# The planner of an attention and max-out FFN kernel gets other step durations, paces and margins

## The chip, the cores and the metric

The kernel runs on one core of one Trainium2 chip. The metric is the device time of one launch in microseconds (us). The median of the runs is given, beside one profiled execution whose trace is read here.

## What is computed

Windowed attention for 8 batches of 8 heads (576 positions, head size 64), followed by an FFN with the maximum of three up projections:

```python
scores = scale * np.matmul(q, k.transpose(0, 1, 3, 2))
rel = pos[:, None] - pos[None, :]
mask_plain = (rel >= 0) & (rel < 32)                       # heads 0 to 3
mask_dil = (rel >= 0) & (rel < 32 * 4) & (rel % 4 == 0)    # heads 4 to 7
scores = np.where(masks[None], scores, -1e9)
attn = np.exp(scores - np.max(scores, axis=-1, keepdims=True))
attn = attn / (np.sum(attn, axis=-1, keepdims=True) + 1e-09)
x = np.matmul(attn, v)                 # to (8 * 576 tokens, 512)
h = np.maximum(np.maximum(x @ w1, x @ w2), x @ w3)   # 512 to 768
out = h @ w_out                                       # 768 to 512
```

All is float32. The kernel keeps that accuracy by splitting each operand of the large products into a high part and a low part (`fp32r`) and adding three products: high by high, high by low, low by high.

## The kernel before

**Attention units.** The 4608 tokens are cut into 16 halves of 288 tokens. A half has four units (`attention(u, wait)`, 64 in all), each a pair of heads: two units with the plain window, two with the dilated one. A unit loads `raw` (its queries and keys) and `v`; casts `raw` to `F` and subtracts for the low parts (`qlow`, `klow`); multiplies (`scores`, tile `s`); adds the mask (`masked`) and reduces (`summed`); takes exponentials with their sums (`expo`, L578); adds 1e-9 and inverts (`eps`, `recip`); normalises (`norm`); transposes on VectorE into `PT` (`turn`, L684); multiplies by `v` (`values`, tile `pv`); and writes the high part `xH` and the low part `xL` of the result. The first 12 units are "lean": they multiply plain float32 on TensorE, with queries laid out in padded tiles `q`, and need no cast. The first eight transpose on TensorE (tile `pt`).

`xH` and `xL` are rings of four halves, so a half can be written only when the up matmuls of the tile that read the half four places earlier are done.

**Weights.** There are 24 up weights (`j` from 0 to 23, four for each of six groups `f` of 128 hidden columns) and 12 down weights. Each arrives as 64-bit words into a staging tile `st` and is put together by a chain: a load on SP; `rebias` (ACT, or DVE) into the PSUM bank `c`; `low3` (POOL, or DVE); `joined` and `sign` on DVE into a tile `c` of the tag `tmp`; `split` into the high part (`wupH` or `wdn`; ACT, DVE or POOL); a subtraction into the low part (`wupL` or `wdn`; POOL, or DVE). Each `rebias` and `low3` follows the `rebias` of the weight before, and the bank `c` has one buffer.

**FFN.** There are 12 tiles of 384 tokens. A tile has 54 up steps of four matmuls (six groups `f`, three projections, three products; tile `u`) and 18 down steps of three matmuls (tile `d`). Between them DVE takes maxima in `tmp`, and ACT and POOL split the result into `h`. Tile 0 needs units 0 to 7 and all weights; tile 1 needs units 8 to 11 too, tile 2 units 12 to 15. Three tiles use up four halves.

**The order.** Every piece of work is a `Step` with a table of engines that may run it and an assumed duration on each; the first is its usual engine. `Plan.deadlines` gives each step a due time: FFN steps on TensorE follow each other at their assumed durations times `FFN_PACE`; the steps before them are dated back along the dependencies, each by its duration times `UNIT_PACE` or `WEIGHT_PACE`, with a margin (`UNIT_SLACK`, `WEIGHT_SLACK`) and a lead per unit or weight ahead of the FFN. FFN steps on TensorE have the due time 1e6 (they fill in behind all attention), FFN steps on other engines -1e3 (they go first). `Plan.order` then simulates the engines with the assumed durations: it always takes the step that can start earliest, and among those the one due first. An engine other than the usual one takes a step only if the usual one would end it more than `SPILL` later. A result is assumed to be ready `AFTER` its engine's duration, and `TO_PE` later for TensorE. A TensorE step after a 3.4 us interval with little work is assumed to take twice as long. The instructions are issued in the order that comes out; on the chip, each engine then runs its own in that order and waits where an input isn't ready.

Of the kernel before, what the change touches and what calls it, by code (L numbers as in the profile page):

```python
# [38 lines left out]

STAGE_F, STAGE_H = 13, 3  # L40

SPILL = 2
TO_PE = 0.26
FFN_PACE = 1.267
UNIT_PACE, UNIT_SLACK, UNIT_LEAD = 1.146, 3.85, 3.484
WEIGHT_PACE, WEIGHT_SLACK, WEIGHT_LEAD = 0.89, 0, 0.8


def blocks_of(hf, dil):
# [54 lines left out]
class Plan:  # L104
# [1 line left out]

    AFTER = {"pe": 0.3, "act": 0.2, "dve": 0.2, "pool": 0.2, "sp": 0.0}

    def __init__(self):
        self.steps = []
# [35 lines left out]
    def order(self):  # L148
        self.deadlines()
        free = {"pe": 0.6, "act": 4.0, "dve": 4.3, "pool": 3.6, "sp": 0.6}  # L150
        wire = 0.0
        busy = {}
        slots = {b.tag: [(0.0, i) for i in range(b.limit)] for st in self.steps for b in st.bufs}
        waiting = {e: [] for e in free}
        for st in self.steps:
            if not st.left:
                for e in st.costs:
                    waiting[e].append(st)
        order = []
        while len(order) < len(self.steps):  # L160
            best = None
            for e, cands in waiting.items():
                now = free[e]
                for st in cands:
                    at = max(now, st.ready[e])
                    if best is not None and at > best[0]:
                        continue
                    for b in st.bufs:
                        if b.slot is None:
                            at = max(at, min(slots[b.tag], default=(1e9,))[0])  # L170
                    if best is not None and (at, st.due) >= best[:2]:
                        continue
                    if e != st.usual:
                        u = st.usual
                        queue = sum(
                            o.costs[u]
                            for o in waiting[u]
                            if o.due < st.due and o.usual == u and o.ready[u] <= at
                        )
                        if max(free[u], st.ready[u]) + queue + st.costs[u] < at + st.costs[e] + SPILL:  # L180
                            continue
                    best = (at, st.due, e, st)
            at, _, e, st = best
            assert at < 1e9, "the steps wait for each other's buffers"
            for b in st.bufs:
                if b.slot is None:
                    free_slot = min(slots[b.tag])
                    b.slot = free_slot[1]
                    slots[b.tag].remove(free_slot)
            if e == "sp":  # L190
                free[e] = at + 0.48
                wire = max(wire, at + 1.1) + st.nbytes / 360e3
                end = wire + 1.0
            else:
                cost = st.costs[e]
                if e == "pe":

                    tick = int(at / TICK)
                    if busy.get(tick - 1, 0) < 3060:
                        cost *= 2  # L200
                    end, cols = at + cost, st.costs[e] * 2400 * st.rows / 128
                    while tick * TICK < end:
                        part = min(end, (tick + 1) * TICK) - max(at, tick * TICK)
                        busy[tick] = busy.get(tick, 0) + cols * part / cost
                        tick += 1
                end = free[e] = at + cost
            st.eng = e
            order.append(st)
            for o in st.costs:
                waiting[o].remove(st)  # L210
            for b in st.bufs:
                b.users -= 1
                b.end = max(b.end, end)
                if not b.users:
                    slots[b.tag].append((b.end + 0.2, b.slot))
            for n in st.next:
                n.left -= 1
                for o in n.costs:
                    if e == o:
                        lat = 0.0 if e == "pe" else 0.13  # L220
                    else:
                        lat = self.AFTER[e] + (TO_PE if o == "pe" else 0.0)
                    n.ready[o] = max(n.ready[o], end + lat)
                if not n.left:
                    for o in n.costs:
                        waiting[o].append(n)
        return order
# [9 lines left out]
def tile_dilated_window_attention__then__maxout_ffn(  # L237
# [49 lines left out]
    plan = Plan()  # L287
# [44 lines left out]
    def tt(eng, dst, a, b, op):  # L332
        (nc.vector if eng == "dve" else nc.gpsimd).tensor_tensor(dst, a, b, op=op)  # L333

    def act(n):
        return 0.15 + 0.00071 * n

    def dve(n):
        return 0.065 + n / 960

    def dve2(n):
        return 0.07 + n / 1920

    def pool1(n):
        return 0.165 + n / 1200

    def pool(n):
        return 0.06 + 0.00235 * n


    NWU = 4 * NF
# [4 lines left out]
    def weight(j, before):  # L356
# [70 lines left out]
            bufs=[st],  # L427
            nbytes=NCH * n,
        )
        first = plan.add({"act": act(n), "dve": dve(n)}, rebias, [s, before], [st, cp])  # L430
        s = plan.add({"pool": pool1(n), "dve": dve(n)}, low3, [s, before], [st])
        s = plan.add({"dve": dve(n)}, joined, [s, first], [st, cp])
        s = plan.add({"dve": dve(n)}, sign, [s], [st, cp, cb])
        s = plan.add({"act": act(n), "dve": dve2(n), "pool": pool1(n)}, split, [s], [cb, *res])
        l = plan.add(
            {"pool": pool(n), "dve": dve(n)},
            lambda e: tt(e, part(1), like(cf()), part(0).bitcast(F32), ALU.subtract),
# [6 lines left out]
    def attention(u, wait):  # L444
# [32 lines left out]
        for j in range(0 if lean else 2):  # L477
            raw, F = buf("raw", f"raw{u}_{j}"), buf("F", f"F{u}_{j}")
            Fs.append(F)

            def load(_, raw=raw, j=j):
                nc.sync.dma_start(out=raw.t[:, :w], in_=qk_src[hf, dil][b, 2 * (p % 2) + j])

            def qlow(e, raw=raw, F=F):
                tt(e, F.t[64:, :HALF], raw.t[64:, :HALF], F.t[64:, :HALF].bitcast(F32), ALU.subtract)

            def klow(e, raw=raw, F=F):
                tt(e, F.t[:, w : w + ksz], raw.t[:, HALF:w], F.t[:, HALF:w].bitcast(F32), ALU.subtract)

            s = plan.add({"sp": 0.5}, load, bufs=[raw], nbytes=512 * w)  # L490
            s = plan.add(
                {"act": act(w), "dve": dve2(w), "pool": pool1(w)},
                lambda e, raw=raw, F=F: copy(e, F.t[:, :w], raw.t[:, :w]),
                [s],
                [raw, F],
            )
            parts.append(
                [
                    plan.add({"pool": pool(HALF), "dve": dve(HALF)}, qlow, [s], [raw, F]),
                    plan.add({"pool": pool(ksz), "dve": dve(ksz)}, klow, [s], [raw, F]),  # L500
                ]
            )
# [22 lines left out]
        for g, grp in enumerate(groups):  # L525
# [50 lines left out]
            def expo(_, n, nk, mo):  # L576
# [3 lines left out]
                )  # L580

            s = plan.add(
                {"pe": sum((4 if lean else 2) * x[3] / 2400 + 0.004 for x in info)},
                scores,
                [x for j in heads for x in parts[j]],
                [bank, *dict.fromkeys(Fs[j] for j in heads), *([qb] if lean else [])],
# [3 lines left out]
            if not lean:  # L590
                nn = sum(x[3] for x in info)
                s = plan.add(
                    {"dve": dve(nn) if info[0][3:] == info[1][3:] else dve(nn) + 0.065},
                    masked,
                    [s],
                    [bank, W],
# [1 line left out]
            for z, (_, i) in enumerate(grp):  # L598
                n, (nk, mo) = n0 + z, blocks[i][3:]
                t = plan.add(  # L600
                    {"dve": dve(nk) + 0.01},
                    lambda _, n=n, z=z, nk=nk, mo=mo, f=summed: f(_, n, z, nk, mo),
                    [s],
                    [bank, W, mx],
                )
                expd.append(
                    plan.add(
                        {"act": act(nk) + 0.15},
                        lambda _, n=n, nk=nk, mo=mo, f=expo: f(_, n, nk, mo),
                        [t],  # L610
                        [W, mx, sm],
# [5 lines left out]
        if not hf:  # L617
# [2 lines left out]
                a = W3() if dil else W.t[:, :768].rearrange("p (j c) -> p j c", j=2)  # L620
                nc.gpsimd.memset(a[:, :, :WIN], 0.0)

            cleared = plan.add({"pool": 0.06 + 0.00088 * (256 if dil else 64)}, clear, [expd[0]], [W])

        PT = buf("PT", f"PT{u}")
        copied, normed = [], []
# [2 lines left out]
        def inverse(n0, n1):  # L629
# [7 lines left out]
            def recip(_):  # L637
                nc.vector.reciprocal(sm.t[:nq, n0:n1], sm.t[:nq, n0:n1])  # L638

            r = plan.add({"pool": 0.075}, eps, expd[n0:n1], [sm])  # L640
            return plan.add({"dve": 0.106}, recip, [r], [sm])

        apart = half < APART
        both = None if apart else inverse(0, 2 * nb)
        for j in range(2):
# [7 lines left out]

            r = inverse(n0, n1) if apart else both
            n = nb * (wk - k0)
            done = plan.add({"pool": 0.06 + 0.00195 * n, "dve": dve(n)}, norm, [r, cleared], [W, sm])
            normed.append(done)
            if not turned:
                bank = buf("pt", f"pt{u}_{j}")
# [4 lines left out]
                            bank.t[:wk, nq * i : nq * i + nq], W3()[:nq, n0 + i], ident[:nq, :nq]  # L664
                        )

                s = plan.add({"pe": nb * (nq / 1200 + 0.003)}, transposes, [done], [W, bank], rows=nq)
                copied.append(
                    plan.add(
                        {"act": act(HALF), "dve": dve(HALF)},  # L670
# [30 lines left out]
                        stop=True,  # L701
                    )

        s = plan.add({"pe": 2 * nb * (nq / 1000 + 0.01)}, values, [vload, *copied], [v, PT, pv], rows=0.8 * wk)
        r0 = (half * HALF) % RING

        def view(ap):
# [19 lines left out]
    def ffn(t0, n, x_of, w_of, prev):  # L727
# [4 lines left out]
        for f in range(NF):  # L732
            tmp, hb = buf("tmp", f"tmp{t0}_{f}"), buf("h", f"h{t0}_{f}")
            for g in range(3):
                bank = buf("ffn", f"u{t0}_{f}_{g}")
                terms = ((wupH, 0, 0), (wupH, 0, 1), (wupL, 1, 0))
                for m, (wt, wz, xz) in enumerate(terms):

                    def up(_, m=m, wt=wt, xz=xz, f=f, g=g, bank=bank):
# [7 lines left out]
                            )  # L747

                    prev = plan.add(
                        {"pe": 4 * n / 2400 + 0.011},  # L750
                        up,
                        [
                            prev,
# [17 lines left out]
                        [bank, tmp],  # L771
                    )
            a = plan.add(
                {"act": act(n), "dve": dve2(n), "pool": pool1(n)},
                lambda e, tmp=tmp, hb=hb: copy(e, hb.t[:, 0, :n], tmp.t[:, :n]),
                [s],
                [tmp, hb],
# [12 lines left out]
        for s0 in range(0, n, 128):  # L790
            bank, o = buf("ffn", f"d{t0}_{s0}"), buf("o", f"o{t0}_{s0}")
            for f in range(NF):

                def down(_, f=f, s0=s0, bank=bank):
# [8 lines left out]

                cols = range(NWU + 2 * f, NWU + 2 * f + 2)
                prev = plan.add(
                    {"pe": 0.649},
                    down,
                    [prev, *hsteps[f], *(x for j in cols for x in w_of[j][:2])],
                    [bank, hs[f], wdn[f]],
# [97 lines left out]
```

## Time and profile before

| | |
|---|---|
| median of 3 runs | 789.0 us (787.82 to 789.14) |
| the profiled execution | 788.89 us, span from first to last instruction 787.1 us |
| TensorE (PE) busy | 737.6 us, 94% of the span |
| VectorE (DVE) busy | 455.6 us, 58% |
| ScalarE (ACT) busy | 383.7 us, 49% |
| GpSimd (POOL) busy | 408.9 us, 52% |
| mean granted TensorE clock | 0.970 of full speed |
| HBM read and written | 62.36 MB and 9.44 MB |

In the trace, a record is one instruction with its start and length; PEld is the loading of weights into TensorE. Names such as `tmp<-u` say what is written from what, with buffer numbers left out. L333, L326 and L328 are the lines of helpers, so subtractions and copies are told apart by their tiles.

### The profile page before, as it was taken

The page shows a single profiled execution, that of the slowest core. Times are in us where ns is not written, and L with a number is a line of the kernel's source. Part 1 is how long each engine was busy: PE and PEld are TensorE (multiplying, and loading weights), DVE is VectorE, ACT ScalarE, POOL GpSimd, SP SyncE. Part 2 cuts the span into 40 slices and gives each one's busy share as a digit, 9 for nine tenths or more (in the row PEclk, how much of TensorE's full clock was granted, in tenths as well). Part 3 has the DMA queues.
Part 4 walks back from the last instruction along what each step waited for, and adds up shares of the span by engine and source line. Part 5 has one row for each costly group of instructions (what it writes and reads, how often), then busy time and mean ns, then how long its engine had stood idle before and what let it go on. Part 6 is the DMA issues. An engine that isn't in the chain of part 4 may idle for free.

```text
span 787.1 us, 14709 instructions
## 1 busy us (share of the span) xinstructions
PE 737.6 (94%) x4724; PEld 673.0 (86%) x4724; DVE 455.6 (58%) x1840; ACT 383.7 (49%) x1323; POOL 408.9 (52%) x586
## 2 busy tenths in 40 slices
PE   6679776999999989999999999999999999999998
PEld 5578764898799789899799798899799899899996
DVE  6779998854886896212886887311887721011110
ACT  7776775772667656311467666511377421111111
POOL 5788998892489567411289576711088411011010
PEclk9969975999999999999999999999999999999999
DMA  6985443432433532300432542300243200100001
GB/s 196 271 255 155 131 144 122 146 95 65 129 95 98 169 101 83 101 1 3 128 106 92 157 127 67 104 28 1 81 123 106 67 29 0 41 1 14 28 1 40
DMA packets 41516, 72.75 MB, mean 92 GB/s; under 512 B 4320, under 2 KB 15584, under 8 KB 41440
## 3 DMA queue, kind: packets, MB, share of 16 engines
q1 hardware_dynamic: 41440, 71.81, 29.9%
q8 instruction: 38, 0.62, 0.3%
q14 instruction: 38, 0.31, 0.1%
HBM read 62.36 MB, written 9.44 MB: 91 GB/s over the span
## 4 chain that ended last, share of the span: by engine, by line
PE 61%; DVE 14%; ACT 4%; POOL 3%; issue 2%; DMA 1%; ACTq 0%; POOLq 0%; DVEq 0%
PE u L741 45%; PE d L796 11%; DVE PT L684 9%; PE s L545 3%; POOL F L333 2%; ACT W L578 2%; PE pv L696 2%; DVE xL L333 1%; ACT F L326 1%; DVE W L572 1%; DVE W L558 1%; POOL W L333 1%; DVE F L333 1%; DMA raw<-in_qk_p_dram 1%; DVE tmp L333 0%
## 5 line engine op out<-in xcount | busy, mean ns | idle before, releaser
L333 DVE TENSOR_TENSOR tmp<-u,tmp 128x384 f32<-128x384 f32 x144 | 80.0, 555 | 235.0 <-PE u L741 231.5
L333 POOL TENSOR_TENSOR F<-raw,F 64x288 fp32r<-64x288 f32 (+2 forms) x193 | 165.5, 858 | 71.0 <-issue 39.2
L578 ACT ACTIVATE W<-W,mx 96x128 f32<-96x128 f32 (+2 forms) x448 | 167.3, 375 | 71.9 <-DVE mx L572 71.2
L333 POOL TENSOR_TENSOR h<-tmp,h 128x384 fp32r<-128x384 f32 x72 | 73.6, 1022 | 225.7 <-ACT h L326 225.0
L741 PE MATMUL u<-xH,wupH 128*128 128x384 f32 x864 | 188.0, 339 | 0.0
L741 PE MATMUL u<-xH,wupL 128*128 128x384 f32 x864 | 187.9, 338 | 0.0
L741 PE MATMUL u<-xL,wupH 128*128 128x384 f32 x864 | 187.8, 338 | 0.0
L796 PE MATMUL d<-wdn,h 128*128 128x512 f32 x648 | 167.1, 404 | 1.3 <-DVE cp L412 0.7
L741 PEld LDWEIGHTS u<-xH,wupH 128*128 128x128 f32 x864 | 152.8, 190 | 1.5 <-issue 0.2
L741 PEld LDWEIGHTS u<-xH,wupL 128*128 128x128 f32 x864 | 152.7, 190 | 0.6 <-POOL wupL L333 0.3
L741 PEld LDWEIGHTS u<-xL,wupH 128*128 128x128 f32 x864 | 152.7, 190 | 0.2
L796 PEld LDWEIGHTS d<-wdn,h 128*128 128x128 f32 x648 | 119.6, 191 | 27.9 <-POOL wdn L333 2.5
L684 DVE STREAM_TRANSPOSE PT<-W 32x192 f32<-32x192 f32 (+1 forms) x336 | 134.7, 401 | 13.8 <-PE pv L696 7.0
L333 POOL TENSOR_TENSOR W<-W,sm 96x384 f32<-96x384 f32 (+2 forms) x121 | 96.7, 811 | 19.9 <-DVE sm L638 13.3
L326 ACT CAST h<-tmp 128x384 fp32r<-128x384 f32 x72 | 36.9, 513 | 143.9 <-DVE tmp L333 143.3
L578 ACT ACTIVATION_READ_ACCUMULATOR W<-W,mx 72x1 f32 (+1 forms) x448 | 85.0, 190 | 0.0
L326 ACT CAST F<-raw 128x576 fp32r<-128x576 f32 (+2 forms) x102 | 72.0, 706 | 9.5 <-DMA raw<-in_qk_p_dram 4.6
L572 DVE CUSTOM_DVE_ANT_0 W<-W,s 96x128 f32<-96x128 f32 (+3 forms) x364 | 75.8, 251 | 1.4
L545 PE MATMUL s<-F 128*96 128x256 f32 (+3 forms) x364 | 60.2, 271 | 16.7 <-DVE mx L572 9.2
L545 PEld LDWEIGHTS s<-F 128*72 128x72 f32 (+1 forms) x364 | 47.0, 154 | 29.6 <-issue 10.9
L558 DVE TENSOR_TENSOR W<-s,mask 72x208 f32<-72x208 f32 (+2 forms) x158 | 53.9, 360 | 25.1 <-PE s L545 23.4
L696 PEld LDWEIGHTS pv<-PT,v 104*64 104x64 f32 (+1 forms) x896 | 38.2, 145 | 32.7 <-issue 13.9
(47 smaller groups left out, 479.6 us busy)
## 6 DMA issues: line engine op xcount, KB each, us to landing
raw<-in_qk_d_dram SPq DMA_DIRECT2D x28, 352.0 KB
st<-in_w_up_dram SPq DMA_DIRECT2D x24, 384.0 KB
out_dram<-o SPq DMA_DIRECT2D x36, 256.0 KB
raw<-in_qk_p_dram SPq DMA_DIRECT2D x28, 304.0 KB
raw<-in_qk_p_dram SPq DMA_DIRECT2D x24, 288.0 KB
raw<-in_qk_d_dram SPq DMA_DIRECT2D x24, 288.0 KB
v<-in_v_d_dram SPq DMA_DIRECT2D x32, 208.0 KB
v<-in_v_p_dram SPq DMA_DIRECT2D x32, 192.0 KB
```

Source lines behind the costliest of these rows:

```text
L326: nc.scalar.copy(dst, src)
L333: (nc.vector if eng == "dve" else nc.gpsimd).tensor_tensor(dst, a, b, op=op)
L545: nc.tensor.matmul(bank.t[:nq, 256 * z : 256 * z + 2 * nk], f[:, q0 : q0 + nq], kv[:, :, k0 : k0 + nk], start=True, stop=True,)
L558: nc.vector.tensor_tensor(W3()[:nq, n0 : n0 + 2, mo : mo + nk], s3[:, :, :nk], m, op=ALU.add)
L572: nc.vector.tensor_tensor_reduce(a, x, y, -0.125, 3e38, ALU.add, ALU.min, mx.t[:nq, n : n + 1])
L578: nc.scalar.activation(a, a, AF.Exp, bias=mx.t[:nq, n : n + 1], scale=-1.0, accum_out=sm.t[:nq, n : n + 1])
L684: nc.vector.transpose(PT.t[c : c + 32, : 2 * nb, 32 * i : 32 * i + 32], W3(e)[32 * i : 32 * i + 32, :, c - e : c - e + 32],)
L696: nc.tensor.matmul(pv.t[64 * j : 64 * j + 64, q0 : q0 + nq], v.t[:wk, j, i, :], PT.t[:wk, nb * j + i, :nq], start=True, stop=True,)
L741: nc.tensor.matmul(bank.t[:, :n], wt[:, 3 * f + g, c, :], (xL if xz else xH)[:, c, r0 : r0 + n], start=(m == 0 and c == 0), stop=(m == 2 a ...
L796: nc.tensor.matmul(bank.t, hs[f].t[:, hz, s0 : s0 + 128], wdn[f].t[:, wz], start=(f == 0 and m == 0), stop=(f == NF - 1 and m == 2),)
```

## The change

The assumed durations, the margin per result (`AFTER`), the assumed DMA rate and the constants of the due times get other numbers. Nothing else of the code differs: the steps, their dependencies, buffers and instructions are the same. The plan made from them can differ in the order of the steps and in the engine of a step that may run on several.

```diff
-SPILL = 2
+SPILL = 2.0
-FFN_PACE = 1.267
-UNIT_PACE, UNIT_SLACK, UNIT_LEAD = 1.146, 3.85, 3.484
-WEIGHT_PACE, WEIGHT_SLACK, WEIGHT_LEAD = 0.89, 0, 0.8
+FFN_PACE = 0.982
+UNIT_PACE, UNIT_SLACK, UNIT_LEAD = 1.754, 6.852, 3.484
+WEIGHT_PACE, WEIGHT_SLACK, WEIGHT_LEAD = 0.535, 26.965, 0.8
...
-    AFTER = {"pe": 0.3, "act": 0.2, "dve": 0.2, "pool": 0.2, "sp": 0.0}
+    AFTER = {"pe": 0.27, "act": 0.12, "dve": 0.06, "pool": 0.12, "sp": 0.0}
...
-                wire = max(wire, at + 1.1) + st.nbytes / 360e3
+                wire = max(wire, at + 1.1) + st.nbytes / 275e3
...
-                        lat = 0.0 if e == "pe" else 0.13
+                        lat = 0.0 if e == "pe" else 0.03
...
-    def act(n):
-        return 0.15 + 0.00071 * n
+    def act(n, psum=True):
+        return (0.155 if psum else 0.195) + 0.00084 * n
     def dve(n):
-        return 0.065 + n / 960
+        return 0.15 + 0.00105 * n
     def dve2(n):
-        return 0.07 + n / 1920
+        return 0.15 + 0.00053 * n
     def pool1(n):
-        return 0.165 + n / 1200
+        return 0.17 + 0.00093 * n
     def pool(n):
-        return 0.06 + 0.00235 * n
+        return 0.08 + 0.00245 * n
...
     scores
-                {"pe": sum((4 if lean else 2) * x[3] / 2400 + 0.004 for x in info)},
+                {"pe": sum(4 * x[3] / 2400 + 0.004 if lean else x[3] * 0.00087 + 0.0062 for x in info)},
     masked, where the two blocks differ
-                    ... dve(nn) + 0.065
+                    ... dve(nn) + 0.14
     summed
-                    {"dve": dve(nk) + 0.01},
+                    {"dve": dve(nk) + 0.07},
     expo
-                        {"act": act(nk) + 0.15},
+                        {"act": act(nk) + 0.33},
     clear
-            {"pool": 0.06 + 0.00088 * (256 if dil else 64)}
+            {"pool": 0.1 + 0.0008 * (256 if dil else 64)}
     eps, recip
-            {"pool": 0.075} ... {"dve": 0.106}
+            {"pool": 0.22} ... {"dve": 0.18}
     norm
-            {"pool": 0.06 + 0.00195 * n, "dve": dve(n)}
+            {"pool": 0.13 + 0.00188 * n, "dve": dve(n)}
     transposes on TensorE
-                {"pe": nb * (nq / 1200 + 0.003)}
+                {"pe": nb * (nq / 1200 + 0.03)}
     values
-        {"pe": 2 * nb * (nq / 1000 + 0.01)}
+        {"pe": nb * nq / 600 + 0.28}
     up
-                        {"pe": 4 * n / 2400 + 0.011},
+                        {"pe": 4 * (n * 0.000435 + 0.0062)},
     down
-                    {"pe": 0.649},
+                    {"pe": 0.686},
```

The casts on ScalarE that read SBUF (`rebias`, `split`, the cast of `F`, the high part of `h`) use `act(n, False)` after the change.

More of the change, by code (lines that the diff above doesn't have):

```diff
@@ L429, in weight @@
         )
-        first = plan.add({"act": act(n), "dve": dve(n)}, rebias, [s, before], [st, cp])
+        first = plan.add({"act": act(n, False), "dve": dve(n)}, rebias, [s, before], [st, cp])
         s = plan.add({"pool": pool1(n), "dve": dve(n)}, low3, [s, before], [st])
@@ L433, in weight @@
         s = plan.add({"dve": dve(n)}, sign, [s], [st, cp, cb])
-        s = plan.add({"act": act(n), "dve": dve2(n), "pool": pool1(n)}, split, [s], [cb, *res])
+        s = plan.add({"act": act(n, False), "dve": dve2(n), "pool": pool1(n)}, split, [s], [cb, *res])
         l = plan.add(
@@ L491, in attention @@
             s = plan.add(
-                {"act": act(w), "dve": dve2(w), "pool": pool1(w)},
+                {"act": act(w, False), "dve": dve2(w), "pool": pool1(w)},
                 lambda e, raw=raw, F=F: copy(e, F.t[:, :w], raw.t[:, :w]),
@@ L592, in attention @@
                 s = plan.add(
-                    {"dve": dve(nn) if info[0][3:] == info[1][3:] else dve(nn) + 0.065},
+                    {"dve": dve(nn) if info[0][3:] == info[1][3:] else dve(nn) + 0.14},
                     masked,
@@ L621, in clear @@
                 nc.gpsimd.memset(a[:, :, :WIN], 0.0)
-            cleared = plan.add({"pool": 0.06 + 0.00088 * (256 if dil else 64)}, clear, [expd[0]], [W])
+            cleared = plan.add({"pool": 0.1 + 0.0008 * (256 if dil else 64)}, clear, [expd[0]], [W])
         PT = buf("PT", f"PT{u}")
@@ L638, in recip @@
                 nc.vector.reciprocal(sm.t[:nq, n0:n1], sm.t[:nq, n0:n1])
-            r = plan.add({"pool": 0.075}, eps, expd[n0:n1], [sm])
-            return plan.add({"dve": 0.106}, recip, [r], [sm])
+            r = plan.add({"pool": 0.22}, eps, expd[n0:n1], [sm])
+            return plan.add({"dve": 0.18}, recip, [r], [sm])
         apart = half < APART
@@ L655, in attention @@
             n = nb * (wk - k0)
-            done = plan.add({"pool": 0.06 + 0.00195 * n, "dve": dve(n)}, norm, [r, cleared], [W, sm])
+            done = plan.add({"pool": 0.13 + 0.00188 * n, "dve": dve(n)}, norm, [r, cleared], [W, sm])
             normed.append(done)
@@ L665, in transposes @@
                         )
-                s = plan.add({"pe": nb * (nq / 1200 + 0.003)}, transposes, [done], [W, bank], rows=nq)
+                s = plan.add({"pe": nb * (nq / 1200 + 0.03)}, transposes, [done], [W, bank], rows=nq)
                 copied.append(
@@ L702, in values @@
                     )
-        s = plan.add({"pe": 2 * nb * (nq / 1000 + 0.01)}, values, [vload, *copied], [v, PT, pv], rows=0.8 * wk)
+        s = plan.add({"pe": nb * nq / 600 + 0.28}, values, [vload, *copied], [v, PT, pv], rows=0.8 * wk)
         r0 = (half * HALF) % RING
@@ L773, in ffn @@
             a = plan.add(
-                {"act": act(n), "dve": dve2(n), "pool": pool1(n)},
+                {"act": act(n, False), "dve": dve2(n), "pool": pool1(n)},
                 lambda e, tmp=tmp, hb=hb: copy(e, hb.t[:, 0, :n], tmp.t[:, :n]),
```

## The prediction

> **What bounds the kernel now.** I read the page first, then busy times by stage, then the chain that ended last, then the instructions of the first 146 us.
>
> ```profile
> span 787.1 us, 14709 instructions
> PE 737.6 (94%) x4724; PEld 673.0 (86%) x4724; DVE 455.6 (58%) x1840; ACT 383.7 (49%) x1323; POOL 408.9 (52%) x586
> ```
>
> Over the whole span TensorE is the bound. The stages differ: below, each row is a stage with the busy us of PE, PEld, DVE, ACT and POOL, then the granted clock. I cut it where tile 0's up matmuls begin, where they end, where tile 1 begins, and around the steady part (tiles 2 to 8).
>
> ```profile
> 0.00:53.00 53.00, 35.22 (x336) 30.75 (x336) 36.99 (x228) 39.74 (x169) 35.93 (x78) 0.88 0.83 246
> 53.00:109.30 56.30, 49.49 (x309) 46.21 (x306) 53.15 (x162) 40.99 (x133) 50.46 (x72) 0.90 0.45 138
> 109.30:146.00 36.70, 26.96 (x144) 19.51 (x143) 32.54 (x140) 25.04 (x88) 32.36 (x50) 0.72 0.51 155
> 206.00:632.00 426.00, 415.49 (x2709) 379.04 (x2707) 273.02 (x1117) 221.36 (x773) 239.03 (x325) 1.00 0.29 89
> ```
>
> From 53 to 146 us DVE and POOL are full (53.15 and 50.46 of 56.3 us) and PE is starved: from 109.3 to 146 us it is busy 26.96 of 36.7 us, and at a clock of 0.72, where it has 1.00 in the part from 206 to 632 us, busy 415.49 of 426.
>
> The chain has tile 10's and 11's pieces without attention between them, and a piece that recurs every three tiles:
>
> ```profile
> 187.25 2.08 PE d L796 x9
> ...
> 369.54 2.08 PE d L796 x9
> ...
> 733.50 37.44 PE u L741 x216
> 770.95 12.39 PE d L796 x54
> ```
>
> A pure tile is 37.44 + 12.39 = 49.83 us: 0.1733 us for an up matmul, 0.2294 for a down one. Three tiles in the steady part take 369.54 - 187.25 = 182.3 us instead of 149.5, for 16 attention units beside them.
>
> The start: PE's own order, with the wait in brackets, and the two weight tiles that POOL finishes last for each weight.
>
> ```profile
> 53.09 1.65 PE L741 MATMUL u<-xH,wupH 128*128 128x384 f32 x4
> ...
> 99.43 1.23 PE L696 MATMUL pv<-PT,v 128*64 128x96 f32 x12 [3.81 <-DVE PT L684]
> ...
> 145.99 0.87 PE L741 MATMUL u<-xH,wupH 128*128 128x384 f32 x4
> ```
>
> ```profile
> L333 POOL TENSOR_TENSOR wupL<-c,wupH x24: 994/1008/1078, 22.0 to 101.5; 128x384 fp32r<-128x384 f32 x24
> ```
>
> ```profile
> L333 POOL TENSOR_TENSOR wdn<-c,wdn x12: 722/731/740, 103.6 to 129.8; 128x256 fp32r<-128x256 f32 x12
> ```
>
> Tile 0 takes 145.99 - 53.09 = 92.9 us for 49.83 us of work, because its weights arrive at (101.5 - 22.0) / 23 = 3.46 us each for the up ones, where PE could use one every 9 x 4 x 0.1733 / 4 = 1.56 us, and (129.8 - 103.6) / 11 = 2.38 us each for the down ones. Meanwhile attention goes on beyond need. Counting pv matmuls (12 or 16 a unit, 14 on average):
>
> ```profile
> 0.00:53.00 53.00, 7.12 (x112) 0.88 0.83 246
> 53.00:109.30 56.30, 4.27 (x72) 0.90 0.45 138
> 109.30:146.00 36.70, 3.89 (x56) 0.72 0.51 155
> ```
>
> 112 + 72 + 56 = 240 is 17 units by 146 us; tile 1 needs 12. Five units went ahead of the down weights that PE was waiting for.
>
> **The change, part by part.** No instruction is added or removed; what can change is the order on the five queues (SP's loads with them) and which of two or three engines takes a step that may run on several. So each price is one of waiting.
>
> *Priorities.* A step's due time breaks ties among steps that could start equally early. I worked the due times out from the diff. An up step of the FFN cost 0.651 x 1.267 = 0.825 and becomes 0.693 x 0.982 = 0.681; nine steps a weight group give 7.42 and 6.12 f. The last step of up weight group f moves from 0.3 + 7.42 f to 6.12 f - 26.5 (less a lead up to 2.4), the last of units 0 to 7 from -14..-4 to -18..-7, of down weights from 43..48 to 8..12, of units 8 to 11 from 45..55 to 31..42. So before, all up weights stood behind units 0 to 7 and the down weights stood among units 8 to 11; after, weight groups 0 to 2 stand among units 0 to 7, and the down weights stand 20 us ahead of units 8 to 11.
>
> What that gives: one weight's chain is serial, since the bank `c` has one buffer and each `rebias` waits for the one before.
>
> ```profile
> L399 ACT ACTIVATE cp<-st 128x384 f32<-128x384 f32 x19 | 9.9, 522 | 4.7 <-DVE c L420 4.5
> L412 DVE SCALAR_TENSOR_TENSOR cp<-cp,st 128x384 uint32<-128x384 uint32 x24 | 13.2, 551 | 0.2
> L420 DVE SCALAR_TENSOR_TENSOR c<-st,cp 128x384 uint32<-128x384 uint32 x24 | 13.1, 545 | 0.3
> ```
>
> 0.522 + 0.551 + 0.545 = 1.62 us, plus, at each of the three visits, half of a foreign instruction of 0.5 us that is under way: 2.4 us, against 3.46 now. Units 0 to 7 still compete, so I take the middle, 2.9: 23 x 0.55 = 12.6 us sooner for the last up weight, and 2.2 instead of 2.38 for the down ones, 2 us. Tile 1 starts 15 us sooner. The bounds: nothing (the weights keep their pace), and 30 us (the DVE time of the five early units, worked out next, is all that can be put off). Below nothing: if weights displace units 0 to 7, the first up matmul comes later than 53. SP's loads are the place: up to 53 us the DMA engines are 0.83 busy and move 246 GB/s, so each weight of 1024 x 384 bytes that is loaded ahead of a unit's `q`, `k` or `v` puts that unit back by 1.6 us; four more such weights are 6 us. But tile 0 is then still paced by its weights, which come sooner, so 6 us is the most that I allow as a loss.
>
> Given back: in the steady stage
>
> ```profile
> 206.00:632.00 426.00, 280.52 (x1512) 1.00 0.29 89
> ...
> 206.00:632.00 426.00, 97.35 (x381) 1.00 0.29 89
> ...
> 206.00:632.00 426.00, 42.59 (x272) 1.00 0.29 89
> ...
> 206.00:632.00 426.00, 28.02 (x544) 1.00 0.29 89
> ```
>
> are u, d, s and pv: 7 tiles and 544 / 14 = 39 units. DVE's 273.0 us less 7 x 12 maxima of 0.555 us (row below) leave 226.4 / 39 = 5.8 us a unit. 15 us of DVE at 0.9 busy are 2.3 units put off. On PE a unit costs 0.65 for pv and seven score matmuls of some 0.09:
>
> ```profile
> 144.31 0.45 PE s L545 x4
> ...
> 169.50 0.27 PE s L545 x4
> ...
> 214.23 0.65 PE pv L696 x12
> ```
>
> that is 1.28 us, now in a stretch where PE is full: 2.3 x 1.28 = 3 us. Net of the start: -12 us.
>
> *Durations.* This is where a reader should look twice: a record's length is not the time for which it holds its engine.
>
> ```profile
> L578 ACT ACTIVATE W<-W,mx 96x128 f32<-96x128 f32 x160 | 63.3, 397 | 33.5 <-DVE mx L572 33.0 <-DVE sm L638 0.3
> L578 ACT ACTIVATION_READ_ACCUMULATOR W<-W,mx 96x1 f32 x192 | 36.4, 189 | 0.0
> L333 DVE TENSOR_TENSOR tmp<-u,tmp 128x384 f32<-128x384 f32 x144 | 80.0, 555 | 235.0 <-PE u L741 231.5 <-ACT W L578 2.4
> L572 DVE CUSTOM_DVE_ANT_0 W<-W,s 96x128 f32<-96x128 f32 x132 | 31.9, 277 | 0.9
> L684 DVE STREAM_TRANSPOSE PT<-W 32x256 f32<-32x256 f32 x168 | 72.9, 434 | 9.0 <-PE pv L696 5.4 <-POOL W L333 0.8
> ```
>
> ```profile
> 234.39 0.39 ACT L578 ACTIVATE W<-W,mx 96x128 f32<-96x128 f32 x1
> ...
> 234.78 0.39 ACT L578 ACTIVATE W<-W,mx 96x128 f32<-96x128 f32 x1
> ```
>
> ```profile
> 233.87 0.28 DVE L572 CUSTOM_DVE_ANT_0 W<-W,s 96x128 f32<-96x128 f32 x1
> ...
> 234.08 0.28 DVE L572 CUSTOM_DVE_ANT_0 W<-W,s 96x128 f32<-96x128 f32 x1
> ```
>
> An exponential with its sum is 0.397 + 0.189 of records but starts every 0.39 us: the old formula gave 0.391, the new one gives 0.593. A `summed` step starts every 0.21 us: old 0.208, new 0.354. The transpose holds DVE 0.434: old 0.332, new 0.419. The up step on PE is 0.693: old 0.651, new 0.693. So PE comes out right, transposes too, and `summed` and exponentials are now too long; 448 of the latter, 0.2 us each, are 90 us of ACT time that the planner believes in and the chip doesn't spend. Relative to PE the old planner put attention's PE steps too early in bursts of transposes, the new one puts them late, with the inputs already there. That takes away waits of PE and costs nothing as long as attention still fits: 16 units of 5.8 us are 93 us of DVE in 182, and a quarter more fits as well.
>
> ```profile
> PE s L545 <- DVE mx L572: 7.0, 8, 1.9
> ```
>
> is PE's largest wait from 206 to 632 us; PE is idle there 426 - 415.49 = 10.5 us. Counted by spacing, 1512 x 0.1733 + 381 x 0.2294 + 272 x 0.09 + 39 x 0.65 = 399 us, so up to 27 us are lost. I take 6 us off, about half of the visible idle; bounds 0 and 20 off, or 12 more (the slow rival).
>
> *Sum.* The profiled execution took 788.9 us for its span of 787.1, 0.1 below the median of 789.0. 788.9 - 12 - 6 = **771 us**.
>
> **Rivals.**
>
> *No change.* The steady part is bound by PE and by the ring of four halves of `xH`: attention may not run further ahead, and 182.3 us a period stays whatever the priorities. If the weights are held by their staging slots, which come free only with the sign step, the start stays too: 787.3 to 790.5. Against it: the five units ahead of the down weights.
>
> *Slower.* The planner now thinks ACT fuller than it is and hands its optional steps (casts of `F`, of `h`, copies of `xH`) to POOL and DVE, and POOL's subtractions to DVE. There the trace has prices far from the model's 0.45 and 0.55 us:
>
> ```profile
> L333 DVE TENSOR_TENSOR F<-raw,F x15: 455/786/1623, 59.5 to 504.4; 64x288 fp32r<-64x288 f32 x8, 128x288 fp32r<-128x288 f32 x4, 128x320 fp32r<-128x320 f32 x2, 128x416 fp32r<-128x416 f32 x1
> L333 DVE TENSOR_TENSOR W<-W,sm x7: 543/947/3083, 100.1 to 476.6; 96x384 f32<-96x384 f32 x7
> ```
>
> Only the shortest are as modelled. With 60 more such moves at 0.79 us, DVE gets 47 us more work, in stretches where it is full; if two thirds reach PE (a guess) it is +31, and with -18 from above +13: 802 us. It decides from some 35 moves (18 / 0.79 / 0.67). Against it: DVE is believed fuller as well, by more per step, so moves to it look dearer. The Trainium skill, in SBUF — State Buffer, section Who interferes with whom, says that a DVE instruction with two SBUF inputs and a GpSimd instruction that reads SBUF lock each other out for a whole instruction; these spreads agree, and by that rule no fixed duration holds in another order, which speaks for this rival.
>
> *Much faster.* The weights reach 2.4 us each, the down ones 2.0: 23 x 1.06 + 11 x 0.38 = 28.6 us sooner, 28.6 x 0.9 / 5.8 = 4.4 units put off, 5.7 us given back; all of PE's visible idle in the steady part, 10 us, goes too: 788.9 - 22.9 - 10 = 756 us. Against it: units 0 to 7 need the same engines at the same time.
>
> **How the numbers follow.** Chances: the forecast (764 to 782) 0.46; much faster (below 764) 0.12; a small gain (782 to 787) 0.12; within 0.2% (1.6 us, about what a measurement of this kernel can tell from no change) 0.08; slower 0.22, of which the moves have 0.15 and a late first tile the rest. So faster 0.70. The range 757 to 795 (the late first tile with no gain is 788.9 + 6) leaves out some 0.05 below and 0.12 above; the forecast's own is 764 to 782.
>
> **What would show it.** Right: the last `wupL` before 95 us and the last `wdn` before 120; tile 1's first up matmul near 131; fewer than 17 units by then; a clock above 0.72 in tile 0's down stage; a three-tile period near 180. Wrong: weights still 3.4 us apart; more than 40 tensor_tensor of `F` and `W` on DVE; a first up matmul after 75 us; periods above 183.

## The result, and the profile after

The changed kernel takes 757.8 us (median of 4 runs, 757.4 to 759.0) against 788.4 us: a ratio of 0.9619, with a 95% interval of 0.9596 to 0.9641. That is 30.6 us less, where the forecast was 18. It lies below the forecast's own 764 to 782, in what the prediction called much faster and gave 0.12, and inside the wider 757 to 795 by less than 1 us.

From the page of the changed kernel, the span and the busy line:

```profile
span 757.3 us, 14686 instructions
PE 729.9 (96%) x4724; PEld 671.7 (89%) x4724; DVE 459.2 (61%) x1847; ACT 381.7 (50%) x1312; POOL 413.2 (55%) x590
```

The work is the same to within a few records (11 fewer on ACT, 7 more on DVE and 4 more on POOL: steps that changed their engine). Its lines lie one further down (L741 became L742). TensorE's (PE's) order at the start, and the last weight tiles, in the same views as those shown of before:

```profile
63.02 1.65 PE L742 MATMUL u<-xH,wupH 128*128 128x384 f32 x4
...
107.31 2.24 PE L797 MATMUL d<-wdn,h 128*128 128x512 f32 x9
...
126.85 0.88 PE L742 MATMUL u<-xH,wupH 128*128 128x384 f32 x4
```

```profile
L333 POOL TENSOR_TENSOR wupL<-c,wupH x24: 994/1002/1022, 13.1 to 82.2; 128x384 fp32r<-128x384 f32 x24
```

```profile
L333 POOL TENSOR_TENSOR wdn<-c,wdn x12: 720/741/891, 85.6 to 112.7; 128x256 fp32r<-128x256 f32 x12
```

Tile 0 starts 10 us later (63.02 instead of 53.09) and is through 19.1 us earlier: tile 1 begins at 126.85 instead of 145.99. The granted clock ahead of tile 0 is lower than before, 0.70 against 0.88. Cut at these points, the busy times by stage read (PE, PEld, DVE, ACT, POOL, then the granted clock):

```profile
0.00:63.00 63.00, 42.65 (x328) 37.01 (x328) 45.56 (x231) 47.77 (x181) 48.04 (x91) 0.70 0.77 239
63.00:107.30 44.30, 44.30 (x292) 42.79 (x291) 38.36 (x121) 30.37 (x103) 39.18 (x63) 0.96 0.46 141
107.30:126.85 19.55, 16.58 (x98) 12.48 (x97) 17.07 (x69) 12.78 (x44) 16.27 (x23) 1.00 0.40 118
```

In tile 0's up stage PE is busy all of 44.30 us, and DVE is no longer full (38.36 us). Ahead of tile 1, 192 pv matmuls begin, which are 13.7 units at 14 each; before the change it was 236, or 16.9 units.

The steady part, first the changed kernel, then the kernel before over the same stretch:

```profile
190.00:600.00 410.00, 410.00 (x2724) 376.93 (x2724) 283.37 (x1154) 221.94 (x773) 239.66 (x324) 1.00 0.31 95
```

```profile
190.00:600.00 410.00, 398.60 (x2610) 362.68 (x2611) 265.26 (x1070) 209.47 (x728) 221.59 (x303) 1.00 0.30 90
PE s L545 <- DVE mx L572: 7.2, 9, 1.9
```

The last row is PE's largest wait there before; the changed kernel has none in the list of that stretch. From tile 5's first up matmul to tile 8's is a period of three tiles: 388.65 to 571.20 us before (182.6 us), 366.14 to 540.96 after (174.8). Both hold the same matmuls: 648 for `u`, 162 for `d`, 112 for `s` and 224 for `pv`.

So of the 30 us between the two profiled spans, 19.1 lie ahead of tile 1 and 10.7 between tile 1 and the end. The latter is net of the units put off: 44 pv matmuls are 3.1 units, at the prediction's 1.28 us each 4.0 us, so the rest of the run itself gained some 15 us.

### The profile page after: what moved, and what is told of

Its sections match the earlier page's. It is cut to its first block, busy times and chain, and to the rows that moved or that the text cites. A ratio compares the mean times of both kernels' runs of the same rounds, so it can differ in the third digit from the quotient of the medians.

```text
span 757.3 us, 14686 instructions
## 1 busy us (share of the span) xinstructions
PE 729.9 (96%) x4724; PEld 671.7 (89%) x4724; DVE 459.2 (61%) x1847; ACT 381.7 (50%) x1312; POOL 413.2 (55%) x590
## 4 chain that ended last, share of the span: by engine, by line
PE 90%; DMA 3%; POOL 2%; DVE 2%; ACT 1%; issue 1%; SPq 0%; POOLq 0%; ACTq 0%; DVEq 0%
PE u L742 59%; PE d L797 20%; PE pv L697 5%; PE s L546 5%; DMA st<-in_w_up_dram 1%; PE s L537 1%; DMA st<-in_w_dn_dram 1%; POOL W L333 1%; DMA k<-in_lean_d_dram 1%; DMA raw<-in_qk_d_dram 1%; ACT W L579 0%; POOL wupL L333 0%; DVE F L333 0%; POOL F L333 0%; POOL st L407 0%
## 5 line engine op out<-in xcount | busy, mean ns | idle before, releaser
L333 POOL TENSOR_TENSOR F<-raw,F 64x288 fp32r<-64x288 f32 (+3 forms) x195 | 169.6, 871 | 73.8 <-issue 37.5
L742 PE MATMUL u<-xL,wupH 128*128 128x384 f32 x864 | 187.5, 338 | 0.0
L742 PE MATMUL u<-xH,wupH 128*128 128x384 f32 x864 | 187.2, 337 | 0.0
L742 PE MATMUL u<-xH,wupL 128*128 128x384 f32 x864 | 186.0, 336 | 0.0
L797 PE MATMUL d<-wdn,h 128*128 128x512 f32 x648 | 164.5, 397 | 0.5 <-POOL wdn L333 0.5
L742 PEld LDWEIGHTS u<-xH,wupH 128*128 128x128 f32 x864 | 151.4, 188 | 1.1
L742 PEld LDWEIGHTS u<-xH,wupL 128*128 128x128 f32 x864 | 151.6, 188 | 0.5
L742 PEld LDWEIGHTS u<-xL,wupH 128*128 128x128 f32 x864 | 151.0, 188 | 0.9
L797 PEld LDWEIGHTS d<-wdn,h 128*128 128x128 f32 x648 | 116.7, 188 | 24.0 <-POOL wdn L333 0.8
L326 ACT CAST F<-raw 128x576 fp32r<-128x576 f32 (+2 forms) x91 | 64.5, 710 | 27.1 <-PE s L546 15.7
L326 ACT COPY tmp<-u 128x384 f32<-128x384 f32 x72 | 34.6, 480 | 48.3 <-PE u L742 48.0
L546 PEld LDWEIGHTS s<-F 128*72 128x72 f32 (+1 forms) x364 | 48.6, 150 | 10.2 <-issue 1.4
```

The lines of the kernel that those rows point to most:

```text
L326: nc.scalar.copy(dst, src)
L546: nc.tensor.matmul(bank.t[:nq, 256 * z : 256 * z + 2 * nk], f[:, q0 : q0 + nq], kv[:, :, k0 : k0 + nk], start=True, stop=True,)
L742: nc.tensor.matmul(bank.t[:, :n], wt[:, 3 * f + g, c, :], (xL if xz else xH)[:, c, r0 : r0 + n], start=(m == 0 and c == 0), stop=(m == 2 a ...
L797: nc.tensor.matmul(bank.t, hs[f].t[:, hz, s0 : s0 + 128], wdn[f].t[:, wz], start=(f == 0 and m == 0), stop=(f == NF - 1 and m == 2),)
```

## The experiments

The table has each run's median, its ratio to the runs of the kernel before on the same chip, and, from PE's order in its trace, the start of tile 1 and the period from tile 5 to tile 8 in us.

| run | us | ratio (95% interval) | tile 1 | period |
|---|---|---|---|---|
| before | 788.4 | 1 | 146.0 | 182.6 |
| after | 757.8 | 0.962 (0.960 to 0.964) | 126.9 | 174.8 |
| 1 weights early | 787.3 | 1.000 (0.998 to 1.002) | 141.1 | 182.1 |
| 2 weights late | 773.4 | 0.982 (0.979 to 0.985) | 144.2 | 174.8 |
| 3 occupancy | 772.4 | 0.981 (0.978 to 0.985) | 129.8 | 179.2 |
| 4 before, new TensorE durations | 796.1 | 1.012 (1.009 to 1.014) | 148.7 | 182.7 |
| 5 weights early, DMA rate | 778.6 | 0.989 (0.987 to 0.991) | 138.3 | 179.9 |
| 6 occupancy, old margins | 759.3 | 0.965 (0.963 to 0.967) | 124.5 | 177.4 |
| 7 durations 10% shorter | 766.7 | 0.975 (0.973 to 0.976) | 129.9 | 176.8 |
| 8 after, old TensorE durations | 762.1 | 0.969 (0.968 to 0.971) | 128.5 | 175.2 |
| 9 paces and TensorE durations | 790.2 | 1.003 (1.001 to 1.004) | 134.6 | 187.7 |
| 10 short steps and transposes | 769.4 | 0.976 (0.973 to 0.978) | 134.8 | 177.5 |
| 11 the same, back to old | 780.4 | 0.990 (0.987 to 0.992) | 131.2 | 186.2 |
| 12 other paces | 761.2 | 0.966 (0.964 to 0.968) | 122.6 | 177.5 |

**1, weights early**: the kernel before with the weights' new due times alone.

```diff
-WEIGHT_PACE, WEIGHT_SLACK, WEIGHT_LEAD = 0.89, 0, 0.8
+WEIGHT_PACE, WEIGHT_SLACK, WEIGHT_LEAD = 0.535, 26.965, 0.8
```

> The kernel before, with only the weights' due times of the change (WEIGHT_PACE 0.535, WEIGHT_SLACK 26.965); all durations and the units' paces are the old ones. Theory A (the start is won by the weights' due times, the steady part by the durations): tile 1's first up matmul at about 130 us instead of 146, three units put off that cost 4 us later, the three-tile period still 182 us: 788 - 16 + 4 = 776 us, within 771 to 781. Rival B (due times only act if DVE and ACT are believed full, so nothing comes of them with the old durations): 785 to 790 us, tile 1 at 142 or later.

No gain: 787.3 us. The weights do come sooner, and tile 1 starts 4.9 us earlier, but tile 0 starts at 68.9 us. The first issues of SP's queue, PE's largest wait over the whole run, and POOL's up and down weights:

```profile
0.75 6.62 SPq L426 DMA_DIRECT2D st<-in_w_up_dram  x4
7.42 0.43 SPq L469 DMA_DIRECT2D k<-in_lean_p_dram  x1
7.89 1.20 SPq L466 DMA_DIRECT2D q<-in_lean_p_dram  x2
```

```profile
PE s L536 <- DMA q<-in_lean_p_dram: 19.4, 2, 11.2
```

```profile
L333 POOL TENSOR_TENSOR wupL<-c,wupH x24: 990/998/1017, 8.0 to 87.5; 128x384 fp32r<-128x384 f32 x24
```

```profile
L333 POOL TENSOR_TENSOR wdn<-c,wdn x12: 729/740/747, 91.1 to 116.0; 128x256 fp32r<-128x256 f32 x12
```

The last down weight is 14 us sooner (116.0 against 129.8), but not because the weights come faster: the up weights are (87.5 - 8.0) / 23 = 3.46 us apart, as before, and the first is 14 us sooner. The weights' loads have gone ahead of the lean units' `q`, for which PE waited 3.7 us in the kernel before. Theory A falls in this form; rival B gave the time but not tile 1's start exactly.

**2, weights late**: the changed kernel with the weights' old due times.

```diff
-WEIGHT_PACE, WEIGHT_SLACK, WEIGHT_LEAD = 0.535, 26.965, 0.8
+WEIGHT_PACE, WEIGHT_SLACK, WEIGHT_LEAD = 0.89, 0, 0.8
```

> The changed kernel, with only the weights' due times put back (WEIGHT_PACE 0.89, WEIGHT_SLACK 0). Theory A: tile 1's first up matmul back at 141 to 146 us instead of 127, the three-tile period stays near 175 us: 758 + 17 - 4 = 771 us, within 766 to 776. Rival B (the start too is won by the durations): 756 to 761 us.

773.4 us, as theory A had it: 15.6 us lost, tile 1 17.3 us later, 2.3 units fewer put off, and the period untouched at 174.8. With the new durations and the units' new paces the weights' due times are worth 15 us; with the old ones (run 1), nothing.

**3, occupancy**: the changed kernel with ACT and DVE near the distance from one start to the next (the edit in short; the addend of `masked` for unlike blocks also goes from 0.14 back to 0.065).

```diff
-    act(n, psum): (0.155 if psum else 0.195) + 0.00084 * n;  expo: act(nk) + 0.33
+    act(n, psum): 0.15 + 0.00071 * n;                        expo: act(nk) + 0.15
-    dve(n): 0.15 + 0.00105 * n;  dve2(n): 0.15 + 0.00053 * n;  summed: dve(nk) + 0.07
+    dve(n): 0.065 + n / 960;     dve2(n): 0.07 + n / 1920;     summed: dve(nk) + 0.01
     turn: 0.16 + 0.00105 * 64 * nb    (0.43 and 0.36 us, near what it was)
```

> The changed kernel, with the durations of ACT and DVE put back to about the distance from one start to the next (the old formulas, 0.39 us for an exponential, 0.21 us for a summed step, and 0.43 us for a transpose of 256); TensorE, POOL, margins and paces stay changed. Theory A (too long durations on ACT and DVE place attention's TensorE steps late, with their inputs there): waits of PE come back, the three-tile period goes from 175 to 178 or more, 763 to 770 us. Rival C (what helps is that durations are true, TensorE's above all): 752 to 759 us.

772.4 us and a period of 179.2: the loss that theory A predicted and somewhat more. The sixth run bears on its reason.

**4, before with the new TensorE durations** (`scores`, transposes on TensorE, `values`, up and down steps as in the change; nothing else).

> The kernel before, with only TensorE's durations of the change (an up step 0.693 instead of 0.651, a down step 0.686 instead of 0.649, and the small ones). Theory A: ACT and DVE are now believed faster still against TensorE, so attention's TensorE steps come no later and the waits stay: 785 to 792 us, period 181 or more. Rival C (TensorE's true durations make the gain of the steady part): 772 to 778 us, period 176 or less.

Rival C falls: 796.1 us, 1.2% slower than before and beyond theory A's range too. Durations near the trace's for the engine that bounds the kernel, with the others left as they were, make the order worse.

**5, weights early with a lower DMA rate, nearer to the trace's** (246 GB/s up to 53 us before).

```diff
-WEIGHT_PACE, WEIGHT_SLACK, WEIGHT_LEAD = 0.89, 0, 0.8
+WEIGHT_PACE, WEIGHT_SLACK, WEIGHT_LEAD = 0.535, 26.965, 0.8
-                wire = max(wire, at + 1.1) + st.nbytes / 360e3
+                wire = max(wire, at + 1.1) + st.nbytes / 280e3
```

> The kernel before with the weights' due times of the change, as in the first experiment, and the assumed DMA rate at 280 GB/s instead of 360 (at 275 the plan's steps wait for each other's buffers). Theory D (in the first experiment the weights' loads were planned at a rate that the DMA engines don't reach, so the lean units' q came late; with a rate near that of the trace the weights' priority pays): TensorE's wait for q under 6 us instead of 19, tile 1's first up matmul at 126 to 133 us instead of 141, 772 to 778 us. Rival E (what holds the start is the too short durations of ACT and DVE): tile 1 at 137 us or later, 782 to 790 us.

Between the two: 778.6 us, tile 1 at 138.3, and PE still waits for `q`:

```profile
PE s L536 <- DMA q<-in_lean_p_dram: 11.6, 1, 11.6
```

Theory D holds only in part: the time is just above its range, and tile 1 comes where rival E had it. The period falls too, from 182.1 to 179.9. Most of the start needs something else.

**6, occupancy with the old margins**: the third run with the margins put back too.

```diff
-    AFTER = {"pe": 0.27, "act": 0.12, "dve": 0.06, "pool": 0.12, "sp": 0.0}
+    AFTER = {"pe": 0.3, "act": 0.2, "dve": 0.2, "pool": 0.2, "sp": 0.0}
-                        lat = 0.0 if e == "pe" else 0.03
+                        lat = 0.0 if e == "pe" else 0.13
```

> The changed kernel with the durations of ACT and DVE near the start-to-start distance, as in the third experiment, and the margins after a result put back too (AFTER 0.3 and 0.2, 0.13 on the same engine), which is nearer to the end of a record plus the hand-over. Theory A (record-long durations help as a margin on the engine's time itself): 763 to 773 us, three-tile period 178 or more. Rival F (short durations were harmless in the third experiment, its fault was the small AFTER): 750 to 759 us, period 175 or less.

759.3 us, at the edge of rival F's range and outside theory A's; the period of 177.4 lies between the two. So the third run's 13 us come back with the margins alone: they were lost by results believed ready too early. A duration up to the next start with a margin for the rest, or a record's whole length with a small margin: both give 758 to 759 us. My reading that the over-long exponentials and `summed` steps are what helps is refuted for the larger part: 5.2 of the period's 7.7 us come without them. The last 2.6 us, and PE's last 3.6 us of idle time in the 410, go only where these steps are believed long (periods of 174.8 in the changed kernel and in run 2, 175.2 in run 8; 177.4 here and 177.5 in run 12), so they may help a little.

**7, all durations on ACT, DVE and POOL times 0.9** in the simulation of the order.

> The changed kernel with all durations on ACT, DVE and POOL times 0.9 in the simulation of the order (due times as changed). Theory A: a part of the margin is gone: the period goes from 175 to 176 or 178, the start gains up to 4 us: 757 to 765 us. Rival F (nearer to the true occupancy is better): 748 to 755 us.

766.7 us, 9 us worse, and out of both theories' ranges. POOL's steps and the transposes, which were near the trace, are then too short too. That this is the reason was not tried by itself, but PE's largest wait over the whole run is now one for POOL:

```profile
PE s L546 <- POOL F L333: 6.2, 7, 2.6
```

**8, the changed kernel with the old TensorE durations.**

> The changed kernel with TensorE's durations of before (6% too short for the FFN). Theory A: against TensorE, ACT and DVE are then believed slower still, attention's TensorE steps come after more FFN steps, no new waits: 755 to 763 us, period 173 to 177. Rival C (true TensorE durations are needed for the steady gain): 766 us or more.

762.1 us, as theory A had it: TensorE's new durations are worth 4 us here (6 by the ratios), and cost 8 in the fourth run.

**9, paces and TensorE durations**: the fourth kernel with all new paces.

> The kernel of the fourth experiment (before with TensorE's durations of the change) with all paces and margins of the due times of the change too; DMA rate and the durations of the other engines are old. Theory G (the paces make the gain, in the steady part too): 760 to 770 us, tile 1 at 130 us or sooner, period 177 or less. Theory H (the paces make the start, the corrected short steps and transposes make the steady part): tile 1 at 128 to 138 us, period 180 to 183, 773 to 784 us.

790.2 us, outside both theories' ranges. Tile 1 starts at 134.6, as theory H said, but the steady part is the worst of all and worse than H had it: a period of 187.7, PE idle 16 of the 410 us below. Against the fourth run the paces bring tile 1 14.1 us forward and the whole 6 us; against the kernel before nothing is left.

```profile
190.00:600.00 410.00, 393.93 (x2565) 357.50 (x2564) 266.06 (x1064) 205.59 (x729) 216.57 (x296) 1.00 0.31 89
PE s L545 <- DVE mx L572: 8.6, 14, 2.6
```

The weights come as soon as in the changed kernel, and PE waits no longer for `q` than in the kernel before (3.7 us there over the whole run):

```profile
L333 POOL TENSOR_TENSOR wupL<-c,wupH x24: 995/999/1451, 13.1 to 83.1; 128x384 fp32r<-128x384 f32 x24
```

```profile
PE s L536 <- DMA q<-in_lean_p_dram: 3.8, 1, 3.8
```

**10, short steps and transposes**: the fourth kernel (796 us) with three more durations; all paces old. The edit in short:

```diff
     turn:   -dve(64 * nb)  +0.16 + 0.00105 * 64 * nb     (0.33 and 0.27 -> 0.43 and 0.36 us)
     eps:    -0.075         +0.22
     recip:  -0.106         +0.18
```

> The kernel of the fourth experiment with, besides, the transposes at 0.43 and 0.36 us instead of 0.33 and 0.27, the addition of 1e-9 at 0.22 instead of 0.075 and the reciprocal at 0.18 instead of 0.106; all paces, the DMA rate and the rest old. Theory H: period 177 or less, tile 1 still at 142 to 149 us, 770 to 779 us. Theory G: period 181 or more, 784 to 798 us.

769.4 us: these three durations are worth some 27 us on top of the fourth run. The period falls from 182.7 to 177.5; time and period miss theory H's figures by half a us each, and theory G's by far more. Tile 1 moves from 148.7 to 134.8 us, sooner than either theory had it, with the weights' old due times. PE's waits from 190 to 600 us:

```profile
190.00:600.00 410.00, 406.73 (x2672) 372.25 (x2669) 272.40 (x1118) 216.84 (x769) 231.10 (x315) 1.00 0.31 91
PE s L545 <- DVE mx L572: 1.4, 3, 0.8
```

**11, the same three back to old** in the sixth kernel (759 us).

> The kernel of the sixth experiment (759 us) with the transposes, the addition of 1e-9 and the reciprocal back at their too short durations; paces, TensorE, POOL and DMA rate stay changed. Theory H: period from 176.7 to 179 or more, 764 to 774 us. Theory G: 757 to 762 us.

780.4 us, 21 us lost, more than theory H had; the wait is back:

```profile
190.00:600.00 410.00, 396.35 (x2582) 361.69 (x2581) 258.50 (x1072) 208.14 (x739) 225.42 (x308) 1.00 0.31 90
PE s L546 <- DVE mx L573: 7.2, 11, 1.5
```

**12, other paces** for the sixth kernel.

> The kernel of the sixth experiment with other paces: FFN_PACE 0.908, UNIT 1.782, 6.187, 3.37, WEIGHT 0.575, 27.612, 0.861, SPILL 1.95, under which its plan ends 5 us sooner, with tile 1 at 111.5 us instead of 118. In the sixth experiment the chip was 19 us behind its plan and 6 us behind it at tile 1. If the plan's gain reaches the chip: 751 to 756 us, faster than the changed kernel's 757.8, tile 1 at 117 to 121 us. If paces are only a draw of luck that the chip mixes anew: 757 to 766 us.

761.2 us, no faster than the sixth or the changed kernel, as the second theory had it. Tile 1 starts 1.9 us sooner than in the sixth run, and 3.2 us are lost after it by the profiled spans, 1.5 of them for the 1.1 units put off. No version here beats the changed kernel.

## Why the prediction was right or wrong

**The start: right in size, partly by luck.** I forecast tile 1 at 131 us, the last up weight before 95, the last down weight before 120, fewer than 17 units, and a clock above 0.72 in tile 0's down stage. It came to 126.9, 82.2, 112.7, 13.7 and 1.00. The term was -15 us and 3 back; it measured -19.1 and 4.0 back. The sum got its 15 us from weights that come closer together. The up weights are now (82.2 - 13.1) / 23 = 3.00 us apart instead of 3.46, which is 10.4 us where the sum had 12.6. The down weights are (112.7 - 85.6) / 11 = 2.46 apart instead of 2.38, a loss of 0.9 where the sum had a gain of 2. The other 8.9 us come from the first up weight, at 13.1 instead of 22.0 us, which the sum left out.

That the due times bring the weights forward holds: without them tile 1 is back at 144.2 (run 2), and all paces together, with ACT, DVE, POOL and the DMA rate as before, bring it 14.1 us forward (run 4 to run 9). What the prediction took too lightly is the price for the units: with the weights' due times alone (run 1) their loads go ahead of the lean units' `q` and tile 0 starts 15.8 us later, where the prediction allowed a loss of 6. Run 9 waits for `q` no longer than the kernel before, at the old DMA rate, so the units' paces and `FFN_PACE`, changed along with the weights', do what run 1 lacked. And one cause wasn't in the prediction at all: the three short durations alone move tile 1 by 14 us with the old due times (run 4 to run 10).

**The steady part: right sign, mis-sized.** I took 6 us, about half of PE's visible idle of 10.5 us, and a period near 180. The period is 174.8. The idle time all went, 410.00 busy of 410, and with the gaps inside PE's records the gain is some 15 us. The mechanism that I put in front, exponentials and `summed` steps believed too long, has at most about a third of the period's gain (run 6). What the runs showed in its place is a term that the prediction read off, put down in half a sentence ("So PE comes out right, transposes too") and gave no price. A transpose holds DVE for its whole record: this row from the kernel before

```profile
223.21 2.67 DVE L684 STREAM_TRANSPOSE PT<-W 32x256 f32<-32x256 f32 x6
```

is six in 2.67 us, 0.445 each, where the old plan assumed 0.332. Six transposes a unit, each believed 0.11 us too short, are 0.7 of a unit's 5.8 us of DVE. The addition of 1e-9 (96x6: 225 ns measured, 0.075 us assumed) and the reciprocal (178 ns, 0.106) add 0.2 us to the chain up to the normalised `W`; these two the prediction didn't look at. So the old plan had the transposes end early, and behind them the next unit's masks and maxima queue on DVE; PE's `scores`, which need the bank that these read, wait for them: `PE s <- DVE mx` is 7.2 us before, 7.2 in run 11, 1.4 in run 10 and gone after. The traces bear the order out. Each of the nine waits of before has six or seven transposes on DVE in the 4.5 us ahead of its end, for example

```profile
265.26 1.79 DVE L684 STREAM_TRANSPOSE PT<-W 32x256 f32<-32x256 f32 x4
267.08 0.28 DVE L572 CUSTOM_DVE_ANT_0 W<-W,s 96x128 f32<-96x128 f32 x1
```

```profile
267.73 0.42 PE L545 MATMUL s<-F 128*96 128x192 f32 x2 [0.78 <-DVE mx L572]
```

and in run 10, none of the three waits has a transpose there. But the transposes aren't the whole of that wait. The two longest of before, 1.95 us each, also have a normalisation of 3.08 us on DVE ahead of the six transposes, where the old plan assumed 0.465 us:

```profile
287.56 3.08 DVE L333 TENSOR_TENSOR W<-W,sm 96x384 f32<-96x384 f32 x1
290.75 2.28 DVE L684 STREAM_TRANSPOSE PT<-W 32x192 f32<-32x192 f32 x6
```

And run 5 has the old transposes and yet only 2.7 us of this wait in the same 410 us, so the rest of the order counts too.

**The rivals.** No change: refuted, the period does depend on the order. Slower by moved steps: it didn't happen. After, DVE has 13 subtractions for `F` (15 before) and 8 normalisations of `W` (7):

```profile
L333 DVE TENSOR_TENSOR F<-raw,F x13: 597/1017/2802, 88.7 to 580.0; 64x288 fp32r<-64x288 f32 x9, 128x288 fp32r<-128x288 f32 x3, 128x320 fp32r<-128x320 f32 x1
L333 DVE TENSOR_TENSOR W<-W,sm x8: 654/997/1240, 148.7 to 473.6; 96x384 f32<-96x384 f32 x6, 72x416 f32<-72x416 f32 x1, 72x288 f32<-72x288 f32 x1
```

The prices stay as bad as read (the shortest `F` takes 0.60 us where the model has 0.45, one takes 2.8 us); their number is what didn't grow. The Trainium skill, in SBUF — State Buffer, section Who interferes with whom, says that a DVE instruction with two SBUF inputs contends with a GpSimd instruction that reads SBUF; these spreads agree with that, but no run here takes GpSimd's part away to show it. The "much faster" case, 756 us, is where the kernel ended, but not by its sum: 19 rather than 29 us at the start, and 15 rather than 10 behind it.

**What stays open.** The transposes, the addition of 1e-9 and the reciprocal were only changed together, and always beside the new TensorE durations; which of the three does most was not tried. How 14 us of the start hang on them was not traced. From run 10 to run 6 (10 us), the paces, the DMA rate and POOL's durations were not taken apart. Each run is one order, and chance has a part in each: two sets of paces with the same durations (runs 6 and 12) differ by 2 us, far less than the 21 and 27 us of runs 11 and 10, but as much as the smallest differences in the table. Runs 6 and after can't be told apart by their intervals.

## What to carry to other kernels

In a kernel whose order comes from a planner, look for the steps whose assumed duration is most wrong per unit of work, on any engine that feeds the bound; here three small ones were worth over 20 us, and new durations for the bounding engine alone cost 8. Check what a record means before it goes into a plan: what counts is when the engine takes the next instruction, and when the result is ready; either the record with a small margin, or the start-to-start distance with a larger one, gave the same time here, and the distance with the small margin cost 13 us. A due time is worth what the rest of the plan allows: the weights' new ones brought 15 us with the new durations and the units' new paces, and nothing with the old ones.

## What was not expected of the hardware

How far records overlap depends on the instruction. Maxima of 128x384 have records of 555 ns, and the next instruction can start after 0.47 us; `summed` steps of 128 start every 0.21 us with records of 277 and 78 ns, and exponentials every 0.39 us with records of 397 and 189 ns; transposes of 32x256 have records of 434 ns and start every 0.445 us, with no overlap at all. And loads that nothing waits for at once can hold up those that something does: 19.4 us of TensorE's time in run 1, when the weights' loads were issued ahead of 72 KB pieces of `q`, against 3.7 us before.
